# A Fourier transform in front of a mixture of experts: folding the input on VectorE in the first three batches too

## The chip, the cores and the metric

The kernel runs on one core of a Trainium2 chip. The metric is the time of one execution on the device in microseconds (us); lower is better. Three executions of the kernel before took 1033.86, 1037.51 and 1032.04 us, so its median is 1033.86 us.

The core has a TensorE (PE, matrix products, with PEld for its weight loads), a VectorE (DVE), a ScalarE (ACT), a GpSimd (POOL, here only an issuer of indirect transfers) and a SyncE (SP, which issues the other transfers). All transfers run on 16 shared DMA engines.

## The reference

The first half takes the real part of a two-dimensional Fourier transform of `x` (8 batches x 2496 positions x 256 features). The second half sends every one of the 19968 resulting rows to one of 8 experts and applies that expert's two matrices:

```python
X = np.fft.fft(x, axis=1); X = np.fft.fft(X, axis=2); x = X.real
logits = x @ w_gate + modality_bias[modality_id]
e_idx = np.argmax(logits, axis=1)
probs = softmax(logits); gate_w = probs[np.arange(N), e_idx]
for e in range(E):                       # 8 experts, D = 256, F = 1024
    mask = e_idx == e
    h = np.maximum(x[mask] @ w1[e], 0.0)
    out[mask] = gate_w[mask, None] * (h @ w2[e])
```

## The kernel before, in words

**A batch.** Each of the 8 batches `b` passes through four steps. `load_x` brings its input in two halves `c` into the tile `XM`. A half holds, for each of its five positions, the input itself (index 0) and its mirrored part (index 1); the two have to be added, since the real part of the transform needs only their sum. `XM` has two buffers, so the next batch's halves can only be loaded when this batch's first step has read them. `fold` then prepares a half, `stage1` multiplies it with a cosine and sine table (L533 to L541), and `stage23` goes through 11 groups `g`: one product into `T2` (L570), a copy by ACT (L512), a second product with the table `e3` (L585), and an eviction that makes a rounded f16 row on ACT (L516) and its remainder on DVE (L517, with the logits copied by L593). `route` computes expert, gate and destination of every row (L630 to L682; the destinations are the tile `dsti`), and 22 indirect transfers of POOL write the rows to the table `xd`, sorted by expert (`scatter`, L708).

**The mirrored half.** In batches below `UB` = 3 the sum is made by TensorE: `stage1` issues two accumulating products for each position (L538, L539), one on each part, and ACT squares both parts to find a scale (L394). In later batches DVE adds the two parts (L397), ACT squares the sum (L398), and `fold` halves the features again.

**The experts.** A block takes 256 rows of one expert: `xT<-xd` reads them transposed (L1077), L1096 is the first product, L1101 (ACT) and L1102 (DVE) split the result in two f16 tiles, L1116 is the second product, L1124 and L1125 write the rows out. The first three blocks need the rows of batch 0 only, the next 13 those of batches 0 and 1, and so on. Blocks start when the first step of batch 2 is through; from there on TensorE alternates between blocks and the remaining batches.

**The weights.** The 16 weight matrices ("units", two for each expert) are split in two f16 halves by the kernel itself: `wload` brings a unit into a buffer `wa` (four buffers), `wfold` folds it on DVE (L834, L835, even units only), `wnorm` finds its scale (16 small products L848 and DVE steps), `whi` rounds on ACT (L869), `wlo` takes the remainder on DVE (L876), and `wstore` writes the result to memory. Units 0 to 5 are made between the steps of batches 0 and 1.

**What sets the order.** A planner orders every engine's instructions when the program is built. `issue_after(x)` keeps what it encloses behind the instruction `x`; `behind` gives a piece of weight work a low priority and such conditions. Names used in them: `m2t` is the last product of `prep_m2`, which makes the tables `m2u`; `acted` and `mark` are the last eviction on ACT and on DVE; `head` is the end of a step of `route`; `expi` is its exponential; `plused` is the first piece of the rows' tails. An engine runs its list strictly in order: an instruction that waits holds all behind it. SP's list holds the loads, the stores of converted weights and the reads `xT`, in one order.

Of the kernel before, what the change touches and what calls it, by code (L numbers as in the profile page):

```python
# [12 lines left out]
F16 = mybir.dt.float16  # L13
# [60 lines left out]
UB = 3  # L74
RV = 1
# [168 lines left out]
class Kernel:  # L244
# [141 lines left out]

    def fold_add(self, b, c):
        n = 4 if b < UB else 2
        if c == 0:
            self.sq = self.fft.tile([P, n], F32, name=f"nst{n}")  # L390
        if b < UB:
            jk = self.wp.tile([P, NH * D], F16, name="xj", bufs=1)
            for h in range(2):
                self.nc.scalar.activation(jk.rearrange("p (i d) -> p i d", i=NH), self.XM[c][:, h], AF.Square, accum_out=self.sq[:, 2 * c + h:2 * c + h + 1])  # L394
            return
        X = self.XM[c][:, 0]
        self.nc.vector.tensor_tensor(X, X, self.XM[c][:, 1], ALU.add)  # L397
        self.nc.scalar.activation(self.XM[c][:, 1], X, AF.Square, accum_out=self.sq[:, c:c + 1])  # L398
# [56 lines left out]
    def scale(self, b):  # L455


        rt = self.rt
        V = self.nc.vector
        eb = rt.tile([P, 1], F32, name="xeb")  # L460
        s = rt.tile([P, 1], F32, name="xsc")
        inv = rt.tile([P, 1], F32, name="xinv")
        self.pow2(self.total(self.sq, self.psf.tile([P, 512], F32, name="psf")), eb, s, 204 if b >= FB else 188, 2.0 if b < UB else 1.0)
        V.tensor_scalar(inv.bitcast(I32), eb.bitcast(I32), float(66 << 23), None, ALU.add)
        il = None
        if b >= FB:
            il = rt.tile([P, 1], F32, name="xil")
            V.tensor_scalar(eb.bitcast(I32), eb.bitcast(I32), float(56 << 23), None, ALU.add)
            V.tensor_tensor(il, eb, self.ml, ALU.mult)
        self.xs, self.nxt = s, (s, il, inv)  # L470

    def fold(self, b, c):
# [11 lines left out]
        if b < UB:  # L484
            self.PQ = self.XM[c][:, :, :, 0:P], self.XM[c][:, :, :, P:D]
            return
# [32 lines left out]
    def stage1(self, b, c):  # L519
# [3 lines left out]
        for h, src in enumerate(self.PQ):  # L523
# [3 lines left out]
            for i0, n in ((0, 3), (3, 2)):  # L527
# [4 lines left out]
                for i in range(n):  # L532
                    o = v[:, :, 12 * i:12 * i + 12]  # L533
                    if b >= FB:
                        for k, (a, w) in enumerate(HL):
                            nc.tensor.matmul(o, src[:, a, i0 + i, :], self.c1h[:, w, i1 + i, :], start=k == 0, stop=k == 2)  # L536
                    elif b < UB:
                        for k in range(2):  # L538
                            self.staged = nc.tensor.matmul(o, src[:, k, i0 + i, :], self.c1[:, i1 + i, :], start=k == 0, stop=k == 1).ins  # L539
                    else:  # L540
                        nc.tensor.matmul(o, src[:, i0 + i, :], self.c1[:, i1 + i, :], start=True, stop=True)  # L541
# [201 lines left out]
    def stream(self):  # L743
# [13 lines left out]
        for b in range(B):  # L757
# [4 lines left out]
            for g, _ in enumerate(self.stage23(b)):  # L762
# [3 lines left out]
                if g == 0 and b + 1 == FB:  # L766
                    self.m2_split()
# [5 lines left out]
                yield self.at(b)  # L773
            if b + 1 == FB:
# [3 lines left out]
            for step in (ORDER0, ORDER1, ORDER2, ORDER)[min(b, 3)]:  # L778
# [4 lines left out]
                elif step == "s":  # L783
                    next(s, None)
                elif step == "f":
                    with ExitStack() as x:
                        if b == 1:
                            x.enter_context(self.tc.issue_after(self.head))
                        if b == 0:
                            x.enter_context(self.tc.issue_after(self.acted))  # L790
                        self.fold(b + 1, 0)
                elif more:
                    with ExitStack() as x:
# [3 lines left out]
                        if b == 0:  # L797
                            x.enter_context(self.tc.issue_after(self.expi))
                        self.fold(b + 1, 1)
# [357 lines left out]
def fft_moe(ctx, tc, t):  # L1157
# [31 lines left out]
    behind(both(k.whi, 0, 1), k.acted)  # L1189
    behind(both(k.wlo, 0, 1))  # L1190
    both(k.wstore, 0, 1)()
    both(k.wload, 4, 5)()
    steps(12 - WHI)
    steps(7)
    behind(both(k.wnorm, 2, 3))
# [124 lines left out]
```

## Time and profile before

| | |
|---|---|
| three executions | 1033.86, 1037.51, 1032.04 us; median 1033.86 |
| the profiled execution | 1035.88 us, of which the span is 1034.1 us |
| PE busy | 1000.7 us (97%) |
| DVE, ACT, POOL busy | 540.5 us (52%), 443.5 us (43%), 367.6 us (36%) |
| chain that ended last | PE 69%, issue 12%, DMA 10%, POOL 4%, DVE 2%, ACT 2% |

The profile gives the execution in 40 slices, the transfers by queue, the instructions by line, and the chain of work that ended last: followed back from the last instruction, at each step to what released it. A busy share is a mean over the whole span. The change lies in the first 90 us, so the stretches there have to be read by themselves.

### The profile page before, as it was taken

The numbers are of one execution on the slowest core, as the hardware profiler recorded it, in microseconds if no ns is written. First come the engines' busy times: TensorE is split into PE (matmuls) and PEld (weight loads), VectorE is DVE, ScalarE is ACT, GpSimd is POOL, SyncE is SP. The second block draws the span as 40 slices with busy tenths as digits, with TensorE's granted clock in tenths as the row PEclk, the third lists the DMA queues.
The fourth block names the chain that finished last, engine by engine and source line by source line (L and its number), as shares of the span: only waits on it lengthen the run. The fifth ranks groups of instructions, "written<-read, shape, count | busy, mean of one in ns | idle before, by whom it ended". The sixth has DMA issues, their size and how long they took to land.

```text
span 1034.1 us, 25844 instructions
## 1 busy us (share of the span) xinstructions
PE 1000.7 (97%) x9910; PEld 904.4 (87%) x9910; DVE 540.5 (52%) x1577; ACT 443.5 (43%) x870; POOL 367.6 (36%) x351
## 2 busy tenths in 40 slices
PE   6989899999999999999999999999999999999996
PEld 6878788898998889999999998888888888889896
DVE  2859866576857558779754347423232322222221
ACT  4775566555643354455533333333232323233232
POOL 0077822135414441744344334335351212121111
PEclk9999999999999999999999999999999999999999
DMA  9837969278558958989766963897788895594891
GB/s 327 332 137 234 363 167 287 58 236 249 166 139 284 321 157 236 287 250 304 233 182 200 248 184 76 260 262 241 174 235 235 255 257 175 159 294 137 225 207 35
DMA packets 149725, 227.65 MB, mean 220 GB/s; under 512 B 116309, under 2 KB 117375, under 8 KB 132695
## 3 DMA queue, kind: packets, MB, share of 16 engines
q1 hardware_dynamic: 133031, 183.75, 61.1%
q0 software_dynamic: 16560, 42.15, 11.8%
q8 instruction: 80, 1.31, 0.5%
q14 instruction: 54, 0.44, 0.2%
HBM read 191.77 MB, written 62.48 MB: 246 GB/s over the span
## 4 chain that ended last, share of the span: by engine, by line
PE 69%; issue 12%; DMA 10%; POOL 4%; DVE 2%; ACT 2%; SPq 1%; POOLq 0%; ACTq 0%
PE psm L1096 30%; PE pso L1116 30%; DMA wa<-w 5%; DMA XM<-x 3%; POOL out L1125 3%; PE psf L565 2%; PE psf L583 2%; PE psf L570 2%; PE psf L536 1%; POOL xd L708 1%; PE psf L585 1%; DMA pack<-c_pack 1%; PE psf L539 1%; DMA xT<-xd 1%; DVE w L876 1%
## 5 line engine op out<-in xcount | busy, mean ns | idle before, releaser
L1096 PE MATMUL psm<-xT,w 128*128 128x256 f16 (+1 forms) x4368 | 454.4, 261 | 10.2 <-DVE H L1102 5.8
L1116 PE MATMUL pso<-w,H 128*128 128x256 f16 x3864 | 450.5, 273 | 0.9 <-ACT ob L1124 0.9
L1096 PEld LDWEIGHTS <-w 128*128 128x128 f16 x4368 | 384.3, 98 | 49.9 <-issue 8.4
L1116 PEld LDWEIGHTS <-H 128*128 128x128 f16 x3864 | 375.3, 98 | 43.7 <-issue 1.1
L1102 DVE SCALAR_TENSOR_TENSOR H<-psm,H 128x512 f16<-128x512 f32 x322 | 219.8, 687 | 334.6 <-ACT H L1101 334.0
L1125 POOL DMA_INDIRECT out<-ob,ig x161 | 164.7, 1023 | 516.9 <-ACT ob L1124 486.8
L1101 ACT ACTIVATE H<-psm 128x512 f16<-128x512 f32 x322 | 190.5, 596 | 229.9 <-PE psm L1096 227.1
L1124 ACT ACTIVATE ob<-pso,gs 128x256 f32<-128x256 f32 x161 | 68.6, 471 | 247.0 <-PE pso L1116 207.5
L708 POOL DMA_INDIRECT xd<-rp,dsti x88 | 101.4, 1152 | 94.3 <-DVE rm L228 49.9
L708 POOL DMA_INDIRECT xd<-rm,dsti x88 | 92.9, 1055 | 41.9 <-issue 18.5
L517 DVE SCALAR_TENSOR_TENSOR T<-psf,T 120x280 f16<-120x280 f32 (+2 forms) x95 | 43.4, 463 | 42.3 <-ACT T L516 42.2
L876 DVE SCALAR_TENSOR_TENSOR w<-wa,wsc,w 128x1024 f16<-128x1024 f32 x32 | 39.9, 1276 | 9.4 <-ACT w L869 9.3
L516 ACT ACTIVATE T<-psf 120x280 f16<-120x280 f32 (+2 forms) x95 | 38.8, 422 | 10.5 <-PE psf L536 5.7
L570 PE MATMUL psf<-m2u,T 128*120 128x280 f32 x132 | 37.2, 403 | 2.2 <-DVE Lg L593 1.5
L539 PE MATMUL psf<-c,XM 128*128 128x132 f32 x240 | 31.5, 294 | 7.0 <-DMA c<-c_c 6.9
L539 PEld LDWEIGHTS psf<-c,XM 128*128 128x128 f32 x240 | 30.4, 204 | 7.1 <-DMA XM<-x 6.9
L583 PE MATMUL psf<-T,pack 120*128 120x145 f16 x330 | 34.7, 224 | 1.5 <-DVE T L517 1.5
L869 ACT ACTIVATE w<-wa,wsc 128x1024 f16<-128x1024 f32 (+1 forms) x24 | 33.4, 1425 | 4.3 <-DVE wsc L405 3.5
L565 PE MATMUL psf<-pack,T 128*120 128x144 f16 (+1 forms) x330 | 31.5, 229 | 0.0
L512 ACT COPY T<-psf 120x280 f32<-120x280 f32 (+2 forms) x57 | 22.7, 407 | 17.1 <-PE psf L570 8.2
L855 ACT ACTIVATE xj<-wa 128x1024 f16<-128x1024 f32 x20 | 21.1, 1054 | 18.0 <-DVE wa L834 9.1
L516 ACT ACTIVATE rp<-psf 128x256 f16<-128x256 f32 x55 | 21.1, 383 | 15.8 <-PE psf L583 11.8
(186 smaller groups left out, 598.0 us busy)
## 6 DMA issues: line engine op xcount, KB each, us to landing
w<-w SPq DMA_DIRECT2D x80, 1028.0 KB
w<-w SPq DMA_DIRECT2D x80, 1024.0 KB
XM<-x SPq DMA_DIRECT2D x14, 1280.0 KB
wa<-w SPq DMA_DIRECT2D x16, 1024.0 KB
out<-ob,ig POOLq DMA_INDIRECT x161, 7.1
XM<-x SPq DMA_DIRECT2D x2, 768.0 KB
xT<-xd SPq DMA_TRANSPOSE x91
xd<-rp,dsti POOLq DMA_INDIRECT x88, 5.2
```

The lines of the kernel that those rows point to most:

```text
L516: self.acted = self.nc.scalar.activation(dst[:, 0], ps, AF.Identity, scale=scale).ins
L539: self.staged = nc.tensor.matmul(o, src[:, k, i0 + i, :], self.c1[:, i1 + i, :], start=k == 0, stop=k == 1).ins
L565: nc.tensor.matmul(oh, T1[h][:, a, g, :], self.m2h[h][:, w], start=h + k == 0, stop=h * k == 2, skip_group_check=True)
L570: nc.tensor.matmul(ps[0:120, 0:280], T1[h][:, g, :], self.m2u[h], start=h == 0, stop=h == 1)
L583: nc.tensor.matmul(ps3[0:P, cols], self.e3h[:, a, j, :], T2[:, w, cols], start=k == 0, stop=k == 2)
L708: i = self.nc.gpsimd.indirect_dma_start(out=self.t["xd"], out_offset=bass.IndirectOffsetOnAxis(ap=at, axis=0), in_=row, in_offset=None, bo ...
L1096: l1 = nc.tensor.matmul(ps[:, q, :], w1v[:, h, kt, ft], xT[:, xs, :], start=k == 0, stop=k == 5).ins
L1101: nc.scalar.activation(H[:, 0, f0:f0 + NF, :], ps, AF.Relu)
L1102: self.mark = V.scalar_tensor_tensor(H[:, 1, f0:f0 + NF, :], ps, 0.0, H[:, 0, f0:f0 + NF, :], ALU.max, ALU.subtract).ins
L1116: nc.tensor.matmul(po[:, tg, :], H[:, hh, ft, tg * P:(tg + 1) * P], w2v[:, wh, ft, :], start=k == 0, stop=k == 23)
L1124: self.ob = nc.scalar.activation(ob, po[:, tg, :], AF.Identity, scale=gs[:, tg:tg + 1]).ins
L1125: ins = nc.gpsimd.indirect_dma_start(out=t["out"], out_offset=bass.IndirectOffsetOnAxis(ap=ig.bitcast(I32)[:, tg, 0:1], axis=0), in_=ob, i ...
```

## The change

The input is folded by DVE in all batches, and the second product of `stage1` and the second square per half are gone. For batch 0 the four parts are added as they are (`PARTS`); for batches 1 and 2 the additions stand behind groups 7 and 9 of the previous batch's `stage23` (`ADDS`), and the squares in front of the previous batch's `route`. `m2_split`, which makes the f16 tables for batches 3 to 7, stands behind batch 0's `stage23`. Unit 1 (the second matrix of expert 0) is converted behind batch 0's routing; its scale is still found before.

```diff
+    def add(self, c, *parts):
+        for i0, i1 in parts or ((0, NH),):
+            X = self.XM[c][:, 0, i0:i1]
+            self.nc.vector.tensor_tensor(X, X, self.XM[c][:, 1, i0:i1], ALU.add)
...
     def fold_add(self, b, c):
-        n = 4 if b < UB else 2
         if c == 0:
-            self.sq = self.fft.tile([P, n], F32, name=f"nst{n}")
-        if b < UB:
-            jk = self.wp.tile([P, NH * D], F16, name="xj", bufs=1)
-            for h in range(2):
-                self.nc.scalar.activation(jk.rearrange("p (i d) -> p i d", i=NH), self.XM[c][:, h], AF.Square, accum_out=self.sq[:, 2 * c + h:2 * c + h + 1])
-            return
+            self.sq = self.fft.tile([P, 2], F32, name="nst")
         X = self.XM[c][:, 0]
-        self.nc.vector.tensor_tensor(X, X, self.XM[c][:, 1], ALU.add)
+        if b >= UB:
+            self.add(c)
+        elif b == 0:
+            self.add(c, *PARTS)
         self.nc.scalar.activation(self.XM[c][:, 1], X, AF.Square, accum_out=self.sq[:, c:c + 1])
...
-                    elif b < UB:
-                        for k in range(2):
-                            self.staged = nc.tensor.matmul(o, src[:, k, i0 + i, :], self.c1[:, i1 + i, :], start=k == 0, stop=k == 1).ins
                     else:
-                        nc.tensor.matmul(o, src[:, i0 + i, :], self.c1[:, i1 + i, :], start=True, stop=True)
+                        self.staged = nc.tensor.matmul(o, src[:, i0 + i, :], self.c1[:, i1 + i, :], start=True, stop=True).ins
...
-                if g == 0 and b + 1 == FB:
-                    self.m2_split()
+                if b + 1 < UB and g in ADDS:
+                    with self.tc.issue_after(self.mark):
+                        self.add(ADDS.index(g))
...
+            if b == 0:
+                with self.tc.issue_after(self.acted), self.tc.issue_after(self.mark):
+                    self.m2_split()
...
+                elif step == "f" and b + 1 < UB:
+                    with self.tc.issue_after(self.acted if b == 0 else self.head):
+                        self.fold(b + 1, 0)
+                        self.fold(b + 1, 1)
+                    self.parts(0)
...
-    behind(both(k.whi, 0, 1), k.acted)
-    behind(both(k.wlo, 0, 1))
-    both(k.wstore, 0, 1)()
-    both(k.wload, 4, 5)()
+    behind(both(k.whi, 0), k.acted)
+    behind(both(k.wlo, 0))
+    k.wstore(0)
+    k.wload(4)
     steps(12 - WHI)
     steps(7)
+    behind(both(k.whi, 1), k.expi)
+    behind(both(k.wlo, 1), k.plused, k.head)
+    k.wstore(1)
+    k.wload(5)
```

On DVE, in the second half of batch 0's `stage23`, the list before read as follows (`w2_0_107` is the converted unit 1, the `rp` are rows, `wsc` and `web` scales):

```order
L859 TENSOR_SCALAR web_315<-web_315 128x1
L878 TENSOR_TENSOR w2_0_107<-web_287,web_315 128x1
L517 SCALAR_TENSOR_TENSOR rp_405<-psf_402,xsc_167,rp_405 128x256
L593 COPY Lg_245<-psf_402 128x16
L876 SCALAR_TENSOR_TENSOR w2_0_107<-wa_208,wsc_316,w2_0_107 128x1024 x2
L517 SCALAR_TENSOR_TENSOR rp_405<-psf_414,xsc_167,rp_405 128x256
```

The same place now (`XM_312` and `XM_314` are the halves of batch 1):

```order
L596 COPY Lg_223<-psf_373 128x16
L391 TENSOR_TENSOR XM_312<-XM_312 128x1280
L411 TENSOR_SCALAR wsc_294<-web_293 128x1
L523 SCALAR_TENSOR_TENSOR rp_376<-psf_386,xsc_157,rp_376 128x256
L596 COPY Lg_223<-psf_386 128x16
L870 TENSOR_SCALAR web_293<-web_293 128x1
L523 SCALAR_TENSOR_TENSOR rp_376<-psf_397,xsc_157,rp_376 128x256
L596 COPY Lg_223<-psf_397 128x16
L391 TENSOR_TENSOR XM_314<-XM_314 128x1280
```

The two remainders of unit 1 have left this place, and the two additions of batch 1 stand in it.

On DVE, where the `rm` rows (the mirrored outputs) of batch 0 are made behind its routing, the list before ended thus, with the fold of unit 4 (L834) as the last:

```order
L228 TENSOR_SCALAR rm<-rp 128x2x2x127
L614 TENSOR_TENSOR bias<-mf,mb 128x176
L615 TENSOR_TENSOR btmp<-mid,mb 128x176
L917 TENSOR_TENSOR sp_st_3_1155<-sp_st_3_1155,sp_ok_3_1153 1x8
L925 SCALAR_TENSOR_TENSOR sp_nd_3_1161<-sp_ok_3_1153,done_99 1x3
L834 TENSOR_TENSOR wa<-wa 128x1024
```

And now:

```order
L229 TENSOR_SCALAR rm<-rp 128x2x2x127
L928 TENSOR_TENSOR sp_st_3_1105<-sp_st_3_1105,sp_ok_3_1103 1x8
L936 SCALAR_TENSOR_TENSOR sp_nd_3_1111<-sp_ok_3_1103,done_99 1x3
L619 TENSOR_TENSOR bias<-bias,btmp 128x176
L887 SCALAR_TENSOR_TENSOR w_0_107<-wa,wsc,w_0_107 128x1024 x2
L889 TENSOR_TENSOR w_0_107<-web 128x1
L845 TENSOR_TENSOR wa<-wa 128x1024
```

The two remainders of unit 1 now stand directly in front of the fold of unit 4.

On SP, the list before between the converted unit 0 (`w_0_104`) and the first table of blocks (`sp_i`):

```order
L883 DMA w<-w_0_104 128x4096
L826 DMA wa<-w 128x2048
L883 DMA w<-w_0_107 128x4112
L826 DMA wa<-w 128x2048
L385 DMA XM<-x 128x2x1280 x2
L1064 TENSOR_LOAD sp_i_1164
```

And now:

```order
L894 DMA w<-w_0_104 128x4096
L837 DMA wa<-w 128x2048 x2
L894 DMA w<-w_0_107 128x4112
L386 DMA XM<-x 128x2x1280 x2
L1075 TENSOR_LOAD sp_i_1114
```

The loads of units 4 and 5 are now neighbours. Unit 5 goes into the buffer of unit 1, so its load, the store of unit 1 and the loads of batch 2's input behind them all stand behind the conversion of unit 1.

## Rows read from the trace of the kernel before

**Rows 1.** Stretches: us; busy us and count of each engine; granted clock, DMA share, GB/s.

```profile
20.50:42.60 22.10, 20.14 (x136) 16.54 (x136) 16.82 (x45) 14.20 (x28) 0.00 (x0) 1.00 0.90 358
...
51.30:85.40 34.10, 30.62 (x243) 26.09 (x243) 22.86 (x117) 24.73 (x45) 23.71 (x23) 1.00 0.37 124
85.40:140.00 54.60, 49.93 (x399) 42.65 (x398) 44.17 (x116) 31.51 (x63) 43.70 (x28) 0.97 0.89 301
140.00:1034.10 894.10, 877.88 (x8960) 797.11 (x8957) 445.13 (x1229) 355.20 (x696) 299.35 (x295) 1.00 0.73 212
```

**Rows 2.** Chain of waits, 50 to 140 us: start, duration in us, and what.

```profile
51.71 7.32 DMA XM<-x
...
79.75 2.39 DMA xd<-rm,dsti
82.36 1.37 SPq L1077
...
89.14 6.86 DMA XM<-x
96.01 28.02 DMA wa<-w
...
131.79 4.46 DMA xT<-xd
136.30 3.76 PE psm L1096 x33
```

**Rows 3.** Timeline of PE: start, us, engine, line, what; idle time before in brackets.

```profile
6.90 7.25 PE L539 MATMUL psf<-c,XM 128*128 128x132 f32 x40 [6.90 <-DMA c<-c_c]
...
41.27 4.68 PE L539 MATMUL psf<-c,XM 128*128 128x132 f32 x40
...
85.63 1.58 PE L1096 MATMUL psm<-xT,w 128*128 128x256 f16 x13
```

**Rows 4.** Timeline of ACT around the conversion of unit 1 and the squares.

```profile
36.14 1.99 ACT L869 ACTIVATE w<-wa,wsc 128x2048 f16<-128x2048 f32 x1
...
41.85 1.26 ACT L394 ACTIVATE xj<-XM 128x1280 f16<-128x1280 f32 x1
43.01 0.19 ACT L394 ACTIVATION_READ_ACCUMULATOR xj<-XM 128x1 f32 x1
```

**Rows 5.** Timeline of DVE from the first weights to batch 0's destinations.

```profile
20.47 1.23 DVE L834 TENSOR_TENSOR wa<-wa 128x1024 f32<-128x1024 f32 x1 [0.82 <-DMA wa<-w]
...
38.16 2.48 DVE L876 SCALAR_TENSOR_TENSOR w<-wa,wsc,w 128x1024 f16<-128x1024 f32 x2 [1.32 <-ACT w L869]
...
41.98 0.48 DVE L517 SCALAR_TENSOR_TENSOR rp<-psf,xsc,rp 128x256 f16<-128x256 f32 x1
42.38 0.16 DVE L593 COPY Lg<-psf 128x16 f32<-128x16 f32 x1
...
50.20 0.18 DVE L682 CAST dsti<-dst 128x22 int32<-128x22 f32 x1
```

**Rows 6.** Timeline of POOL: batch 0's scatters, then two of batch 1's.

```profile
51.32 1.17 POOL L708 DMA_INDIRECT xd<-rp,dsti  x1 [49.89 <-DVE rm L228]
52.80 0.97 POOL L708 DMA_INDIRECT xd<-rp,dsti  x1 [0.30 <-issue]
54.07 1.70 POOL L708 DMA_INDIRECT xd<-rp,dsti  x1 [0.30 <-ACT T L512]
...
79.75 1.03 POOL L708 DMA_INDIRECT xd<-rm,dsti  x1 [0.30 <-issue]
84.75 10.30 POOL L708 DMA_INDIRECT xd<-rp,dsti  x1 [3.97 <-ACT T L512]
...
100.22 1.78 POOL L708 DMA_INDIRECT xd<-rp,dsti  x1 [0.30 <-issue]
```

**Rows 7.** Timeline of DVE beside those scatters.

```profile
53.70 1.21 DVE L834 TENSOR_TENSOR wa<-wa 128x1024 f32<-128x1024 f32 x1
...
84.50 3.65 DVE L876 SCALAR_TENSOR_TENSOR w<-wa,wsc,w 128x1024 f16<-128x1024 f32 x3
...
99.68 1.47 DVE L397 TENSOR_TENSOR XM<-XM 128x1280 f32<-128x1280 f32 x1
```

More of the change, by code (lines that the diff above doesn't have):

```diff
@@ L74 @@
 UB = 3
+ADDS = 7, 9
 RV = 1
@@ L385, in fetch_x, with parts @@
         self.nc.sync.dma_start(self.XM[c][:, :, i0:i1], self.t["x"][b, :, :, NH * c + i0:NH * c + i1])
+    def add(self, c, *parts):
+        for i0, i1 in parts or ((0, NH),):
+            X = self.XM[c][:, 0, i0:i1]
+            self.nc.vector.tensor_tensor(X, X, self.XM[c][:, 1, i0:i1], ALU.add)
+    def parts(self, c):
+        self.PQ = tuple(self.XM[c][:, 0, :, i:i + P] for i in (0, P))
     def fold_add(self, b, c):
-        n = 4 if b < UB else 2
         if c == 0:
-            self.sq = self.fft.tile([P, n], F32, name=f"nst{n}")
-        if b < UB:
-            jk = self.wp.tile([P, NH * D], F16, name="xj", bufs=1)
-            for h in range(2):
-                self.nc.scalar.activation(jk.rearrange("p (i d) -> p i d", i=NH), self.XM[c][:, h], AF.Square, accum_out=self.sq[:, 2 * c + h:2 * c + h + 1])
-            return
+            self.sq = self.fft.tile([P, 2], F32, name="nst")
         X = self.XM[c][:, 0]
-        self.nc.vector.tensor_tensor(X, X, self.XM[c][:, 1], ALU.add)
+        if b >= UB:
+            self.add(c)
+        elif b == 0:
+            self.add(c, *PARTS)
         self.nc.scalar.activation(self.XM[c][:, 1], X, AF.Square, accum_out=self.sq[:, c:c + 1])
@@ L462, in scale @@
         inv = rt.tile([P, 1], F32, name="xinv")
-        self.pow2(self.total(self.sq, self.psf.tile([P, 512], F32, name="psf")), eb, s, 204 if b >= FB else 188, 2.0 if b < UB else 1.0)
+        self.pow2(self.total(self.sq, self.psf.tile([P, 512], F32, name="psf")), eb, s, 204 if b >= FB else 188)
         V.tensor_scalar(inv.bitcast(I32), eb.bitcast(I32), float(66 << 23), None, ALU.add)
@@ L484, in fold @@
         if b < UB:
-            self.PQ = self.XM[c][:, :, :, 0:P], self.XM[c][:, :, :, P:D]
+            self.parts(c)
             return
@@ L788, in stream @@
                             x.enter_context(self.tc.issue_after(self.head))
-                        if b == 0:
-                            x.enter_context(self.tc.issue_after(self.acted))
                         self.fold(b + 1, 0)
@@ L796, in stream @@
                         self.bias(b + 1)
-                        if b == 0:
-                            x.enter_context(self.tc.issue_after(self.expi))
-                        self.fold(b + 1, 1)
+                        if b + 1 < UB:
+                            self.parts(1)
+                        else:
+                            self.fold(b + 1, 1)
                     for _ in s:
```

## The prediction

> **What bounds the kernel now.** I read the stretches first, then the chain of waits, then the timelines of single engines. In the last 894 us TensorE is busy for 877.88 us [rows 1]: it idles 16 us there, so whatever shifts the start of that stretch shifts the end by as much. What TensorE does before is another matter. Between 51.3 and 85.4 us it idles 3.5 us, and between 85.4 and 140 us another 4.7 us, while the DMA engines are 89% busy [rows 1]. The chain of waits shows who is waited for there, and hardly a link of it is a product of `stage1`: batch 0's last scatter starts at 79.75 us and has landed at 82.14, SP issues the first read `xT` at 82.36, and, because SP's list is in order, the load of batch 3's input only at 89.14; a weight load issued at 96.01 us then lands at 124.03, and the read for the second set of blocks, issued at 131.79, lets TensorE go on at 136.30 [rows 2]. TensorE's first block starts at 85.63 us [rows 3], 3.3 us after the first read was issued. So the first 136 us are set by the moment at which batch 0's 22 scatters are through, and behind that by transfers queued in SP's order. That moment is the sum of three steps: the end of batch 0's `stage23` on VectorE (42.54 us), its routing up to the destinations (50.38 us) [rows 5], and POOL's scatters (51.32 to 80.78 us) [rows 6].
>
> **The change, part by part.** *Products and squares removed.* The 40 records of 20 products take 4.68 us in batch 1 and 7.25 us at the very start [rows 3]; 120 records go, so TensorE loses 3 x 4.68 = 14 us of work or a little more. ACT loses six squares of 1.26 + 0.19 us [rows 4], 8.7 us. Both lie before 85.6 us, where neither engine sets the end. Their gain is worth only what it takes off the three steps; I cost it there and nowhere else.
>
> *Batch 0 up to the end of `stage23`.* VectorE, idle at the start, adds the four parts as they arrive; TensorE has half the products, and may begin `stage23` up to about 3 us earlier. But the first weights still land at 20.47 us [rows 5], and from there on VectorE has the folds, the remainders of unit 0 and 22 evictions in one list. It was busy for 16.82 of the 22.1 us up to 42.6 [rows 1]. From this list the two remainders of unit 1 go (2.48 us, and a wait of 1.32 us ahead of them for ACT's rounding, itself 1.99 us [rows 4, 5]), and two additions of 1.47 us [rows 7] come: 16.82 - 2.48 + 2.94 = 17.3 us of work. With no idle time left it would end at 37.8 us, with all of the 5.3 us kept at 43.1 us. I take 41.3 us, 1.2 us earlier than now, since most of the idle time is waiting for evictions that ACT and TensorE hand over one group at a time, and the additions stand between these.
>
> *Routing of batch 0.* It took 50.38 - 42.54 = 7.84 us. Into its list on VectorE come the eight steps of `m2_split`, the four of batch 1's scale and one of a weight's scale. The trace has such steps at 0.16 us (the small copy) and 0.48 us (the eviction) [rows 5]; eight small and five large ones are 3.7 us at most, and below nothing is excluded, because the routing is a closed row of dependent steps on the same engine. On ACT the two squares of batch 1 (2.9 us) stand ahead of a rounding that `m2_split` needs on VectorE. Overlap lets me take 1.9 us. The destinations then come at 41.3 + 7.84 + 1.9 = 51.0 us, 0.6 us later than now.
>
> *The scatters of batch 0.* A scatter takes 0.97 us and the next follows after 0.30 [rows 6]. The one at 54.07 us took 1.70 us and ended at 55.77, 0.86 us after the fold (53.70 + 1.21 us) in which it began; the one at 100.22 us took 1.78 us and ended 0.85 us after an addition like those that are added here (99.68 + 1.47 us); and the one at 84.75 us, which began in a row of remainders, took 10.30 us [rows 6, 7]. So a scatter that begins while such a step runs waits for its end. Where the fold of unit 4 stood alone, 2.48 us of remainders now stand in front of it: 3.7 us in a row. A scatter begins somewhere in it, on the mean half a spacing (0.64 us) after its start: a wait of 3.1 us instead of 0.73, that is 2.3 us more. The two additions for batch 2, which also fall among these scatters, cost 1.47 - 0.64 = 0.8 us each. Together 4.0 us; the bounds are 0 (each scatter begins just ahead of such a step) and 3.7 - 0.73 + 2.94 = 5.9 us. The first read comes 0.6 + 4.0 = 4.6 us later, at 87.0 us, and TensorE's first block near 90.2 us.
>
> The Trainium skill, "SBUF — State Buffer", section "Who interferes with whom", says that a VectorE step with two inputs in SBUF contends with GpSimd instructions that read SBUF, and infers that writing descriptors needs only the write side, so that additions would leave such transfers alone. By that inference the 4.0 us would be 0; the scatters at 54.07 and 100.22 us say otherwise. It is the second rival below.
>
> *What stands in SP's list.* Unit 5's load, the store of unit 1 and batch 2's input now wait for unit 1's remainders. These end near 51.0 + 6.3 = 57.3 us (the `rm` rows and small steps stand between). 1.05 + 1.05 + 2.62 MB (from the tiles' shapes) at the 358 GB/s of the stretch from 20.5 us [rows 1] are 13.2 us: batch 2's second half lands near 70.5 us, where it landed at 59.03 [rows 2]. Its addition stands behind group 9 of batch 1's `stage23`, which VectorE reaches near 72 us. I cost this at nothing; the slack is 1.5 us.
>
> *What comes through.* Everything behind the first reads in SP's order moves by 4.6 us, up to the read of 131.79 us. The other condition of that read, batch 1's scatters, began at 84.75 us and stood 10.30 us in the remainders; they now begin near 87 us, in the same remainders, so about 2 us later. TensorE's 4.7 idle us in this stretch can take up a little. Between 2 and 4.6 us I take 4.0, near the chain that ended last. Behind 140 us nothing gives it back.
>
> **Sum.** The profiled execution was 1035.88 us, 2.0 us above the median but within the runs. 1035.88 + 4.0 = 1039.9 us for it, and 1033.86 + 4.0 = **1037.9 us** for the median, 0.4% slower: within the 0.5% (5.2 us) that a measurement of this kernel can tell from no change.
>
> **Rivals.** *Batch 2's input comes too late (slower).* The place is SP's list behind unit 1. If the 4.7 MB move at 250 GB/s rather than 358, they need 18.9 us, the second half lands at 76.2 us, and VectorE stands 4 us in the middle of the evictions of batch 1. Its routing, its scatters and the read of 131.79 us follow: 4.6 + 4 = 8.6 us less what TensorE's idle time absorbs, some 1041.5 us. It decides from a landing later than 72 us. For it: the transfers were 90% busy in this part of the kernel before 42.6 us; against it: only 37% from 51.3 to 85.4 us [rows 1].
>
> *Additions and remainders leave the scatters alone.* Then 0.6 us is all: 1034.5 us. Against it are the rows above.
>
> *The early start comes through (faster).* If VectorE works without idle time, batch 0's `stage23` ends at 37.8 us; if `m2_split` hides in the routing, the destinations come at 45.6 us, 4.7 us earlier; if few scatters are held, the reads follow 4 to 6 us earlier, and TensorE has the work taken away to let it. Less the steps of `m2_split` that no longer stand between the first blocks, that is some 6 us: 1028 us. For it: 5.3 us idle on VectorE in that stretch [rows 1], and a wait of 1.32 us that goes with unit 1. Against it: three things have to hold together.
>
> **How the numbers follow.** The forecast has a chance of 0.50, with a range of its own from 1035 to 1041 us; 0.38 of it lies within 0.5% and 0.12 above. The late input has 0.24, the scatters left alone 0.10, the early start 0.16. So faster 0.16, within 0.5% 0.38 + 0.10 = 0.48, slower 0.12 + 0.24 = 0.36. The range that leaves out no more than a tenth at either side reaches from 1030 to 1043 us.
>
> **What would show it.** In the changed kernel's profile: batch 0's last eviction on VectorE near 41 us and its destinations near 51 us; one scatter of about 4 us beside the remainders of unit 1 and two of 1.5 to 2.4 us beside the additions; the first `xT` issued near 87 us and TensorE idle for some us ahead of its first block; the second set of blocks near 140 us; no wait of the additions for batch 2's input. Destinations before 47 us, or scatters of 0.97 us throughout, would make it wrong on the fast side; an addition that waits over 2 us for its input on the slow side.

## The result and the profile after

Over 20 executions each the changed kernel takes 1040.66 us (1037.59 to 1045.36) and the kernel before 1034.86 us (1032.04 to 1037.75): a ratio of 1.0056, 95% interval 1.0044 to 1.0067. The forecast was +4.0 us, the result is +5.8 us. Medians and ratios, here and in the table of the experiments, leave out three executions that took far longer than the others of their kernel (1212.63 us of e2_u1only, 2674.98 us of e5_u1back_rp6, 4106.49 us of the kernel before). The profiled execution of the changed kernel took 1038.10 us, the third fastest of its 20 and only 2.2 us above the profiled one of before; the rows below can account for those 2.2 us, and not for the other 3.6.

The stretches of the changed kernel, with the columns of [rows 1]: length, busy us (and count) of PE, PEld, DVE, ACT and POOL, granted clock, DMA share, GB/s.

```profile
20.50:42.60 22.10, 19.57 (x131) 16.24 (x130) 20.02 (x59) 15.32 (x38) 0.00 (x0) 0.96 0.84 333
42.60:51.30 8.70, 8.69 (x80) 7.73 (x78) 7.71 (x45) 5.14 (x11) 2.09 (x3) 0.90 0.05 16
51.30:85.40 34.10, 24.28 (x151) 20.07 (x152) 20.92 (x79) 20.36 (x36) 24.41 (x20) 0.90 0.63 217
85.40:140.00 54.60, 49.32 (x386) 42.66 (x385) 44.16 (x130) 30.36 (x59) 42.67 (x28) 0.94 0.88 297
140.00:1036.20 896.20, 881.21 (x8984) 799.40 (x8981) 447.98 (x1235) 357.23 (x702) 300.12 (x295) 1.00 0.73 212
```

Against [rows 1], VectorE idles 2.1 us up to 42.6 us instead of 5.3, the DMA engines all but stand still from 42.6 to 51.3 us (16 GB/s) and carry 217 instead of 124 GB/s in the stretch behind, and TensorE idles 9.8 us there instead of 3.5. Its granted clock, a mean over the two levels 1.2 and 2.4 GHz, is below full (1.00) in all four stretches up to 140 us; before, it was so only in the fourth, at 0.97. Behind 140 us it is 1.00 in both, but TensorE has 8984 records of products left there instead of 8960.

VectorE of the changed kernel (start, us, engine, line, what; idle time before in brackets), against [rows 5, 7]:

```profile
38.53 0.47 DVE L523 SCALAR_TENSOR_TENSOR rp<-psf,xsc,rp 128x256 f16<-128x256 f32 x1
38.92 0.16 DVE L596 COPY Lg<-psf 128x16 f32<-128x16 f32 x1
...
47.51 0.16 DVE L685 CAST dsti<-dst 128x22 int32<-128x22 f32 x1
...
51.43 2.46 DVE L887 SCALAR_TENSOR_TENSOR w<-wa,wsc,w 128x1024 f16<-128x1024 f32 x2
...
53.89 1.20 DVE L845 TENSOR_TENSOR wa<-wa 128x1024 f32<-128x1024 f32 x1
...
65.01 0.48 DVE L523 SCALAR_TENSOR_TENSOR rp<-psf,xsc,rp 128x256 f16<-128x256 f32 x1 [6.37 <-ACT rp L522]
...
72.14 1.48 DVE L391 TENSOR_TENSOR XM<-XM 128x1280 f32<-128x1280 f32 x1
...
75.31 1.49 DVE L391 TENSOR_TENSOR XM<-XM 128x1280 f32<-128x1280 f32 x1 [0.24 <-DMA XM<-x]
```

Batch 0's `stage23` ends at 39.08 us and its destinations stand at 47.67, 3.5 and 2.7 us earlier than before. The row at 65.01 is new: 6.37 us in which VectorE waits for ACT's half of the same row (`rp`).

POOL of the changed kernel, against [rows 6]:

```profile
48.60 1.12 POOL L711 DMA_INDIRECT xd<-rp,dsti  x1 [47.17 <-DVE btmp L618]
50.02 0.97 POOL L711 DMA_INDIRECT xd<-rp,dsti  x1 [0.30 <-issue]
51.30 4.68 POOL L711 DMA_INDIRECT xd<-rp,dsti  x1 [0.30 <-ACT T L518]
...
72.97 1.50 POOL L711 DMA_INDIRECT xd<-rm,dsti  x1 [0.30 <-issue]
...
76.05 1.60 POOL L711 DMA_INDIRECT xd<-rm,dsti  x1 [0.31 <-issue]
...
80.53 0.97 POOL L711 DMA_INDIRECT xd<-rm,dsti  x1 [0.30 <-issue]
88.21 9.23 POOL L711 DMA_INDIRECT xd<-rp,dsti  x1 [6.71 <-ACT T L518]
```

The scatter of 51.30 takes 4.68 us and ends 0.89 us after the fold (53.89 + 1.20), the last of a row of remainders and fold; those of 72.97 and 76.05 lie across the two additions. Batch 0's train takes 32.9 us (48.60 to 81.50) instead of 29.5.

The chain of waits of the changed kernel (start, us, what), against [rows 2]:

```profile
50.80 0.40 ACT T L518
...
51.30 13.11 DMA xd<-rp,dsti
...
65.31 1.30 PE psf L588 x4
...
78.61 3.97 ACT w L880 x3
82.58 1.25 ACT XM L404 x2
...
84.64 3.84 PE psf L544 x20
88.48 2.82 PE psm L1107 x24
...
93.90 16.07 DMA wa<-w
...
133.22 3.84 DMA xT<-xd
...
137.11 2.93 PE psm L1107 x13
```

The held scatter needs 13.11 us to land. Of these, 4.68 are the hold on POOL. The other 8.4 fall together with the load of unit 5, the store of unit 1 and batch 2's input, which waited for unit 1's remainders and go out together from 54 us on. The trace has the landing of every scatter: the one of 56.28 us, held by nothing (0.97 us on POOL), lands 8.80 us after its start, while the two of 48.60 and 50.02 us, ahead of those loads, landed after 2.59 and 2.45. So the landing is stretched without a hold too. Batch 1's second buffer `rp` is the one from which the held scatter reads (five buffers, four used by batch 0). So ACT and VectorE stand until 64.4 us, batch 1's `stage23` ends at 78.9 us instead of 76.5, and three roundings and a square on ACT hold the last products ahead of the first block. The first read `xT` is no longer what the first block waits for.

TensorE ahead of the first block, in the changed kernel:

```profile
84.50 3.98 PE L544 MATMUL psf<-c,XM 128*128 128x132 f32 x20
88.27 4.00 PE L1107 MATMUL psm<-xT,w 128*128 128x256 f16 x33
```

and at the same place before:

```profile
80.91 4.77 PE L539 MATMUL psf<-c,XM 128*128 128x132 f32 x40
```

Half of the products now take 3.98 instead of 4.77 us, and no wait stands ahead of the block, which starts at 88.27 us (before: 85.63 [rows 3]). The granted clock was 0.61 from 84.5 to 88.3 us, and 1.00 from 80.9 to 85.6 us before.

A second profiled execution of the same kernel, taken beside the experiments (1037.83 us), has the steps later: last eviction ending at 41.00, destinations at 49.59, the scatter 4.67 us long, the idle row 5.80 us. SP and PE in it:

```profile
86.19 1.37 SPq L1088 DMA_TRANSPOSE xT<-xd  x1
```

```profile
85.96 3.86 PE L544 MATMUL psf<-c,XM 128*128 128x132 f32 x20
89.61 3.56 PE L1107 MATMUL psm<-xT,w 128*128 128x256 f16 x28
```

VectorE takes up the first half `H` of the second set of blocks at 138.43 us in the kernel before, at 141.97 and 142.85 in the two profiles of the changed one. The ways there differ. TensorE's first product of that set starts at 136.30 us before, at 137.11 in the first profile and at 139.97 in the second. In the first profile TensorE had idled 3.93 us for the read, and the clock stood at the lower level behind it:

```profile
137.10:139.10 2.00, 1.99 (x10) 1.44 (x10) 1.79 (x8) 2.00 (x4) 1.70 (x2) 0.50 1.15 194
```

Its first 36 products took 5.45 us there, against 4.09 before and in the second profile.

### The profile page after: what moved, and what is told of

It reads as the page before. It is cut to its first block, busy times and chain, and to the rows that moved or that the text cites. A ratio compares the mean times of both kernels' runs of the same rounds, so it can differ in the third digit from the quotient of the medians.

```text
span 1036.2 us, 25588 instructions
## 1 busy us (share of the span) xinstructions
PE 994.1 (96%) x9784; PEld 895.4 (86%) x9784; DVE 548.1 (53%) x1585; ACT 436.2 (42%) x858; POOL 370.1 (36%) x351
## 4 chain that ended last, share of the span: by engine, by line
PE 68%; issue 12%; DMA 11%; POOL 3%; ACT 2%; DVE 2%; SPq 1%; POOLq 0%; ACTq 0%; DVEq 0%
PE psm L1107 30%; PE pso L1127 29%; DMA XM<-x 3%; DMA wa<-w 3%; POOL out L1136 2%; PE psf L573 2%; DMA xd<-rp,dsti 2%; PE psf L568 2%; PE psf L586 2%; DMA xd<-rm,dsti 1%; PE psf L542 1%; PE psf L588 1%; PE psf L544 1%; ACT w L880 1%; POOL xd L711 1%
## 5 line engine op out<-in xcount | busy, mean ns | idle before, releaser
L711 POOL DMA_INDIRECT xd<-rp,dsti x88 | 105.0, 1194 | 93.0 <-DVE btmp L618 47.2
L391 DVE TENSOR_TENSOR XM<-XM 128x1280 f32<-128x1280 f32 (+2 forms) x18 | 24.1, 1337 | 24.4 <-DMA XM<-x 24.4
L544 PE MATMUL psf<-c,XM 128*128 128x132 f32 x120 | 22.4, 355 | 9.6 <-DVE XM L391 7.7
L544 PEld LDWEIGHTS psf<-c,XM 128*128 128x128 f32 x120 | 20.3, 256 | 12.5 <-DVE XM L391 7.2
L588 PE MATMUL psf<-T,pack 120*128 120x145 f32 (+1 forms) x132 | 23.3, 296 | 5.8 <-ACT T L518 5.7
```

The costliest lines, as they stand in the source:

```text
L544: self.staged = nc.tensor.matmul(o, src[:, i0 + i, :], self.c1[:, i1 + i, :], start=True, stop=True).ins
L711: i = self.nc.gpsimd.indirect_dma_start(out=self.t["xd"], out_offset=bass.IndirectOffsetOnAxis(ap=at, axis=0), in_=row, in_offset=None, bo ...
```

## The experiments

Theory P (pile-up): unit 1 behind the routing holds a scatter and bunches the transfers, and the wait for `rp` carries that to the end. Theory A: only the hold of the scatters counts. Theory C: the lost products let TensorE idle and its clock fall. Three chips (I, II, III) took the twelve runs. Ratios are to the kernel before on the same chip; the clock is the mean over the executions.

| run | chip | this, us | before, us | ratio, 95% interval | clock, this / before |
|---|---|---|---|---|---|
| c_after | I | 1043.09 | 1036.1 | 1.0066, 1.0045 to 1.0087 | 0.986 / 0.996 |
| e1r_u1back | I | 1043.34 | 1036.1 | 1.0072, 1.005 to 1.0094 | 0.987 / 0.996 |
| e3r_rp6 | I | 1042.33 | 1036.1 | 1.0066, 1.0044 to 1.0089 | 0.986 / 0.996 |
| e5_u1back_rp6 | I | 1044.48 | 1036.1 | 1.0082, 1.0055 to 1.0108 | 0.986 / 0.996 |
| e1_u1back | II | 1084.67 | 1086.9 | 0.9984, 0.997 to 0.9998 | 0.972 / 0.978 |
| e2_u1only | II | 1098.80 | 1086.9 | 1.0117, 1.0097 to 1.0137 | 0.973 / 0.978 |
| e3_rp6 | II | 1083.46 | 1086.9 | 0.9978, 0.9953 to 1.0003 | 0.973 / 0.978 |
| e4_xm2first | II | 1090.63 | 1086.9 | 1.0047, 1.0027 to 1.0068 | 0.971 / 0.978 |
| e6_u1back_710 | III | 1088.37 | 1085.9 | 1.0023, 1.0002 to 1.0044 | 0.970 / 0.977 |
| e7_rp6_68 | III | 1086.37 | 1085.9 | 1.0002, 0.9985 to 1.002 | 0.971 / 0.977 |
| e8_twice_610 | III | 1095.58 | 1085.9 | 1.008, 1.0054 to 1.0106 | 0.974 / 0.977 |
| e9_adds_710 | III | 1095.57 | 1085.9 | 1.0088, 1.0065 to 1.0111 | 0.967 / 0.977 |

On chips II and III the kernel before itself takes 4.8 to 4.9% longer than on chip I. The profiles taken there, all of changed versions, have stretches in which ScalarE starts nothing and for whose end the profile names no cause. The chain of waits of e8_twice_610 has the longest:

```profile
68.22 0.39 ACT T L518
68.62 18.72 another core or an unknown queue
```

Its engines in that stretch, in the columns of [rows 1]:

```profile
68.60:87.30 18.70, 1.71 (x8) 1.13 (x8) 0.84 (x6) 0.02 (x1) 12.11 (x13) 0.66 0.56 215
```

Only POOL's scatters and the transfers go on. The chain of e1_u1back has three in a row:

```profile
67.55 6.20 another core or an unknown queue
...
74.24 3.06 another core or an unknown queue
...
77.77 5.34 another core or an unknown queue
```

They lie just where the disputed waits of 3 to 6 us lie, and differ from kernel to kernel. Of these three chips, the changed kernel unedited ran on chip I alone. So the times of chips II and III are told, but no theory is decided by them; what they are used for is the clock ahead of 50 us, where no such stretch has yet come (the earliest begins at 59.88 us).

**Unit 1 back (e1_u1back, e1r_u1back).**

```diff
-    behind(both(k.whi, 0), k.acted)
-    behind(both(k.wlo, 0))
-    k.wstore(0)
-    k.wload(4)
+    behind(both(k.whi, 0, 1), k.acted)
+    behind(both(k.wlo, 0, 1))
+    both(k.wstore, 0, 1)()
+    both(k.wload, 4, 5)()
...
-    behind(both(k.whi, 1), k.expi)
-    behind(both(k.wlo, 1), k.plused, k.head)
-    k.wstore(1)
-    k.wload(5)
```

> The changed kernel with one part undone: unit 1's conversion, store and the next load stand again beside unit 0's; the additions on VectorE and the early M2 split stay. Theory P (pile-up): what the change loses comes from unit 1 behind the routing. It holds the scatter of 51.30 for 4.68 us and sends the store, the load and batch 2's input into the DMA engines just while that scatter lands (13.1 us), so batch 1's fourth rp buffer comes 6.4 us late. P expects no wait of 6 us before batch 1's fourth group of evictions, its second stage's end back at 77 us or earlier, first block products at 85.6 or earlier, and 1031 to 1035.5 us, no slower than the kernel before. Theory C (clock): the loss comes from the half of the stage-1 products that is gone, because TensorE idles more ahead of the blocks and is granted a lower clock. C expects the granted clock of 42.6 to 85.4 us still near 0.9 and 1038 to 1041 us.

> The changed kernel with unit 1 converted beside unit 0 again, on the same chip as the changed kernel itself. On the chip of the first four runs ScalarE stood still several times for 3 to 6 us between two instructions with nothing outstanding that the profile shows, so its profile told nothing of waits of that size. Theory P (pile-up behind unit 1) expects 0.4 to 0.8% less than the changed kernel and at most 1.0 of the kernel before, no wait above 2 us for an rp buffer, and the second stage of batch 1 over by 77 us. Theory C (clock, from the products that are gone) expects a time within 0.2% of the changed kernel.

On chip I the waits that theory P names are gone. POOL of e1r_u1back:

```profile
54.58 2.23 POOL L711 DMA_INDIRECT xd<-rp,dsti  x1 [0.30 <-ACT rp L522]
...
82.10 0.97 POOL L711 DMA_INDIRECT xd<-rm,dsti  x1 [0.31 <-issue]
...
114.69 0.97 POOL L711 DMA_INDIRECT xd<-rm,dsti  x1 [0.30 <-issue]
```

None of batch 0's scatters takes over 2.3 us, VectorE idles at most 1.2 us ahead of an `rp` eviction, batch 1's `stage23` ends at 74.7 us, and its scatters are through at 115.7 us (before: 129.1). But TensorE gains nothing by it. Its first block, which P expected at 85.6 us or earlier, starts later than in the changed kernel, and waits for the first read `xT` (issued at 84.64 us; 82.36 before):

```profile
89.47 6.33 PE L1107 MATMUL psm<-xT,w 128*128 128x256 f16 x36 [4.78 <-DMA xT<-xd]
```

The granted clock was 0.62 from 89.47 to 95.6 us; the same 36 products took 4.09 us in the kernel before. The read for the second set goes out no earlier than before either (131.79 us), though the scatters are through 13 us sooner; here the chain of waits leads to it through a weight load:

```profile
100.56 25.51 DMA wa<-w
```

```profile
132.04 1.29 SPq L1088 DMA_TRANSPOSE xT<-xd  x1
```

VectorE takes up the first `H` of that set at 138.69 us, 0.3 us from the kernel before, but TensorE has 8990 records of products left behind 140 us, as in the changed kernel (8984 and 8996) and not as before (8960). More is lost behind 140 us:

```profile
85.40:140.00 54.60, 46.30 (x364) 39.33 (x364) 43.79 (x107) 29.11 (x55) 29.36 (x25) 0.94 0.89 299
140.00:1047.80 907.80, 886.55 (x8990) 802.61 (x8988) 444.95 (x1235) 355.99 (x701) 304.71 (x297) 0.99 0.72 210
```

The last stretch is 13.7 us longer than in [rows 1]: 8.7 us more busy time of TensorE, 5.0 us more idle (this execution, 1049.6 us, was the slowest of its ten; if the difference to the median 1043.34 lies in this stretch, some 7 us are an estimate for the median). One cause in sight is the planner: with unit 1 back it writes another order for the batches behind. I compared TensorE's products from the first block on, some 9350, row by row as the traces show them (operation, names, shapes): 821 rows differ from the changed kernel's, where only 89 of the changed kernel's differ from those of before. Between the 37th and the 38th `H` of ACT it runs 47 products where there were 12, and batch 2's destinations come at 237.8 us instead of 226.3 (changed kernel: 229.5). How much of the loss is the order's is not shown. So P holds for the waits and falls for the first block and for the time: it expected 0.4 to 0.8% less than the changed kernel, and C's expectation, a time within 0.2% of it, is what came (1043.34 and 1043.09 us). An edit of one part is not an edit of one part when a planner orders the rest.

**Six `rp` buffers (e3_rp6, e3r_rp6).**

```diff
-RPB = 5
+RPB = 6
```

> The changed kernel with six rp buffers instead of five, so that batch 1's fourth group of rows asks for no buffer whose scatters of batch 0 still have to land before; nothing else is edited. Theory P (pile-up, through the rp buffer) expects the wait of 6.37 us at 65.01 gone or under 2 us, batch 1's second stage to end 3 to 6 us earlier than 78.9, the first block then held by the scatters alone (first xT near 82), and 1034 to 1037.5 us. Theory A (only the hold of the scatters counts) expects no change against the changed kernel: 1039.5 to 1041.5 us, since the held scatter of 4.68 us is still there.

> The changed kernel with six rp buffers, on the same chip as the changed kernel itself. Theory P through the rp buffer: the wait of 6.37 us goes, 0.3 to 0.6% less than the changed kernel, about 1.0 of the kernel before. Theory A (only the hold of the scatters counts): within 0.2% of the changed kernel. If the wait goes and the time stays, batch 1's routing was not what set the end, and the hold of the scatters was.

The 6.37 us row is gone, as P says. VectorE of e3r_rp6 then waits for what stood next, batch 2's input:

```profile
71.02 1.49 DVE L391 TENSOR_TENSOR XM<-XM 128x1280 f32<-128x1280 f32 x1 [4.32 <-DMA XM<-x]
...
75.23 1.49 DVE L391 TENSOR_TENSOR XM<-XM 128x1280 f32<-128x1280 f32 x1 [1.27 <-DMA XM<-x]
```

This is the first rival of the prediction at its own place, and it had been hidden only by the longer wait. The second set's first `H` comes at 141.29, 1.6 us earlier than in c_after; the time is the same (1.0066), under another order again (745 rows differ from the changed kernel's). By the words set down for it, a wait that goes and a time that stays speak for theory A; with the order changed as well, that is not shown either.

**Both (e5_u1back_rp6).** The two edits together.

> The changed kernel with both: unit 1 converted beside unit 0 again and six rp buffers. Theory P expects no rp wait even with unit 1 back, so no gain of the sixth buffer over unit 1 back alone: within 0.2% of that kernel, and 0.997 to 1.0 of the kernel before. If the buffer is a wait of its own that the pile-up only made longer, this kernel is 0.2 to 0.4% faster than with unit 1 back alone.

1.0082 beside 1.0072: the sixth buffer gains nothing where unit 1 does not pile up; the order of TensorE's products is the same in both. That half of P's expectation held, the 0.997 to 1.0 did not.

**The changed kernel again (c_after).** No edit.

> The changed kernel itself, unedited, as the yardstick beside the three that follow. All theories expect 1.004 to 1.007 of the kernel before, with the 4.7 us scatter, the rp wait of 6 us and the lower granted clock between 42.6 and 85.4 us again. A time within 0.2% of the kernel before would say that the loss hangs on the chip it runs on.

1.0066, with the 4.67 us scatter, the idle row of 5.80 us and a granted clock of 0.81 and 0.90 in the two stretches from 42.6 to 85.4 us: the loss stays on a chip on which the kernel before takes 1036.1 us.

**Unit 1 alone (e2_u1only).** The kernel before with unit 1's lines (the diff of e1_u1back backwards).

> The kernel before with one part of the change alone: unit 1 converted, stored and its buffer reloaded behind batch 0's routing; the mirrored half still added by matmuls and the M2 split at its old place. Theory P (pile-up) expects a scatter of batch 0 held for 4 us or more beside unit 1's remainders, one that lands in 10 us or more, and a wait of several us for an rp buffer in batch 1's second stage: 1038 to 1043 us. Theory C (clock, from the missing products) expects TensorE as busy as before in 20 to 51 us, a clock of 0.98 or more there, and 1034 to 1036 us.

1.0117 on chip II is above what P expected (1038 to 1043 us are 1.003 to 1.008 of the kernel before) and above C's. The held scatter beside unit 1's remainders took 2.94 us, not 4; the first scatter of batch 1 took 12.68. The clock is 1.00 from 20 to 51.3 us, where every kernel with half the products is below that, so this run loses without C's cause. Its order is not that of before, though (901 rows differ), and its stretches without work (up to 5.90 us) lie where the waits would.

**Batch 2's input first (e4_xm2first).**

```diff
-    k.wstore(1)
-    k.wload(5)
     behind(both(k.wnorm, 2, 3))
     steps(10)
-    behind(both(k.wfold, 4, 5), k.rowed)
+    behind(both(k.wfold, 4), k.rowed)
     steps(12)
+    k.wstore(1)
+    k.wload(5)
+    k.wfold(5)
```

> The changed kernel with unit 1's store and unit 5's load behind batch 2's input in SyncE's list instead of ahead of it; conversion of unit 1 stays behind the routing. Theory P expects the transfers of 51 to 70 us to be spread differently but to be as many: the scatter issued near 51.3 lands in 6 to 10 us instead of 13.1, the rp wait shrinks to 1 to 4 us, 1036 to 1039.5 us. Theory A (only the hold of the scatters counts) expects 1039.5 to 1041.5 us. A third reading, that batch 2's input is what comes late, expects the additions of batch 2 several us earlier and a first block 1 to 2 us earlier.

1.0047 on chip II; its stretches without work (up to 7.29 us) cover the waits in question, and 735 rows of the order differ from the changed kernel's. Inconclusive.

**Four runs with the later order kept.** The places of batch 1's additions (`ADDS`) were chosen so that TensorE's order behind the first blocks stays near that of the changed kernel (27 to 131 rows differ in the traces) or, for the last, of the kernel before (113). e6_u1back_710 is unit 1 back with `ADDS = 7, 10`, e7_rp6_68 six buffers with `ADDS = 6, 8`. The other two:

```diff
 e8_twice_610
-ADDS = 7, 9
+ADDS = 6, 10
...
-                        self.staged = nc.tensor.matmul(o, src[:, i0 + i, :], self.c1[:, i1 + i, :], start=True, stop=True).ins
+                        for k in range(2 if b < UB else 1):
+                            self.staged = nc.tensor.matmul(o, src[:, i0 + i, :], self.c1[:, i1 + i, :], start=True, stop=True).ins
 e9_adds_710 (unit 1's lines as in e1_u1back, and)
-ADDS = 7, 9
+ADDS = 7, 10
...
+                if g == 0 and b + 1 == FB:
+                    self.m2_split()
...
-            if b == 0:
-                with self.tc.issue_after(self.acted), self.tc.issue_after(self.mark):
-                    self.m2_split()
```

> Unit 1 converted beside unit 0 again, as in the second run of that kind, but with batch 1's additions behind the eighth and eleventh group of the second stage (places 7 and 10), because the planner then leaves the order of TensorE's work behind the first blocks as it is in the changed kernel; with 7 and 9 it also rewrote the order of batches 2 and 3, so those runs compared two things at once. Theory P (pile-up behind unit 1) expects the second set of blocks 3 to 5 us earlier than in the changed kernel, and 0.998 to 1.002 of the kernel before. Theory C (the granted clock, lower because TensorE lost half of its stage-1 products) expects the mean clock still near 0.987 and 1.004 to 1.007.

> Six rp buffers again, with the additions at places 6 and 8, which keeps the later order of the changed kernel. Theory P through the rp buffer expects the wait of 6.4 us gone, the second set 1 to 3 us earlier than in the changed kernel, and 1.001 to 1.004 of the kernel before. Theory A (the hold of the scatters alone) and theory C (clock) expect 1.005 to 1.007.

> The changed kernel, unit 1 behind the routing, with each stage-1 product of the first three batches issued twice into the same place, the second overwriting the first, so that TensorE has as many products there as in the kernel before; additions at places 6 and 10, which keeps the later order of the changed kernel. Theory C (clock) expects the granted clock back at 0.99 or more in 20 to 51 us, a mean of 0.993 or more, and 0.999 to 1.002 of the kernel before. Theory P (pile-up) expects the rp wait of some 6 us still there, the second set 2.5 to 5 us late, and 1.004 to 1.008.

> The kernel before with the additions on VectorE alone (half the stage-1 products gone): unit 1 beside unit 0 and the M2 split at its old place; places 7 and 10 keep the later order of the kernel before. Theory P expects no loss, since nothing stands behind the routing: 0.996 to 1.001 of the kernel before. Theory C expects most of the loss to be here: mean clock 0.99 or less, and 1.003 to 1.006.

They came to chip III, so their totals decide little. Taken by their numbers, 1.0002 for six buffers is below P's range (1.001 to 1.004; the interval reaches into it) and below that of A and C; 1.0023 for unit 1 back is just above P's; 1.008 with the products doubled is against C and at the upper end of P's; 1.0088 for the additions alone is against P and above C's. One thing can be read: the clock. A stretch of e8_twice_610, with the products doubled, and then of e9_adds_710, with half of them:

```profile
20.00:42.60 22.60, 18.77 (x124) 15.45 (x125) 16.68 (x41) 13.18 (x32) 0.00 (x0) 1.00 0.84 336
```

```profile
20.00:42.60 22.60, 19.09 (x126) 15.66 (x125) 18.77 (x44) 14.22 (x27) 0.00 (x0) 0.96 0.91 361
```

In 20 to 42.6 us the clock is 0.93 to 0.97 in all eleven profiles with half the products, on all three chips, and 1.00 in the three with all of them (before, e2_u1only, e8_twice_610). So it is the missing products that lower it there. That this makes the time is not shown: from 42.6 to 51.3 us e8_twice_610 falls to 0.80 all the same, its mean (0.974) rises only halfway to that of before, and it is no faster.

No version beats the kernel before on chip I. The held scatter, the stretched landing and the wait for `rp` are shown as waits; that they make the time is not shown, since the two edits that take them away on chip I leave the time where it was and change the order as well.

## Why the prediction was right, step by step

*Products and squares removed.* 14 us of TensorE's work was to go, worked out as 40 records in 4.68 us. The page has TensorE busy 994.1 us instead of 1000.7, 6.6 us less: the 20 records of the row at 84.50 took 3.98 us, under a clock of 0.61. The forecast had costed this gain at nothing outside the three steps, so its sum does not change; that the removed work takes clock with it was in no term.

*The end of `stage23`.* 41.3 us was forecast, 39.08 and 41.00 were measured, inside the bounds of 37.8 and 43.1. VectorE's idle time up to 42.6 us fell from 5.3 to 2.1 us in the first profile and 3.8 in the second.

*The routing.* 9.74 us were forecast (7.84 + 1.9), 8.59 measured in both executions (39.08 to 47.67, 41.00 to 49.59). The steps of `m2_split` cost 0.75 us more than before, not 1.9. The destinations came at 47.67 and 49.59, not 51.0.

*The scatters.* +4.0 us was forecast for the train, +3.4 and +4.6 measured (32.9 and 34.1 us against 29.5). This is the term on which the forecast rested, and its mechanism stands: one scatter of 4.68 us across unit 1's row, and two across the additions (1.50 and 1.60 in one execution, 2.26 and 1.96 in the other). The forecast counted one held scatter in the kernel before, that of 54.07 us; the one of 56.07 took 1.65 us as well, a small error in the sum. The rows also answer the rival from the Trainium skill, "SBUF — State Buffer", section "Who interferes with whom", by whose inference additions would leave these transfers alone: here they do not. The same section has a step with two inputs in SBUF contend with GpSimd instructions that read SBUF; if writing an indirect transfer reads its destinations `dsti` there, that rule covers these rows, but no run here tells whether it does. One-input steps in f16 (the `rm` rows, 49.87 to 51.1 us) left the scatter of 50.02 at 0.97 us.

*The first read and the first block.* 87.0 and 90.2 us were forecast; 83.08 and 88.27 came in one execution, 86.19 and 89.61 in the other. So the path of the forecast, destinations plus scatters, delayed the first read by 0.7 and 3.8 us and not by 4.6. That the first block is near the forecast is luck, for it is late for another reason than the one given: batch 1's `stage23`, late by the `rp` wait, and ACT's list behind it hold TensorE, not the scatters.

*SP's list.* Costed at nothing; this step failed. Batch 2's second half was to land near 70.5 us, and landed at 75.3, beyond the 72 us from which the first rival was to decide. That the additions hardly waited for it (0.24 and 0.60 us) is luck: VectorE came late itself, by the `rp` wait, and with six buffers the wait appears (4.32 and 1.27 us). It was also wrong that the bunched transfers cost nothing else: they stretch the landing of the held scatter to 13.1 us, and with it the turn of the buffer `rp`. I had asked who waits for each transfer of the list and not who waits for the scatters beside it. The rival's rate of 250 GB/s was nearer than 358: the 4.7 MB took 21.2 us, from 54.05 to 75.3, which are 222 GB/s.

*What comes through.* 4.0 us at the second set was forecast, 3.5 and 4.4 measured at its first `H`. In the first profile this is luck in part: the read of that set is 1.4 us late and its first product 0.8, and the rest is the lower clock and VectorE's other work ahead of that `H`; in the second the read is 4.6 us late and the first product 3.7. Counted in work, TensorE has 24 and 36 more records of products left behind 140 us; at 877.88 us for 8960 records [rows 1] these are an estimated 2.4 and 3.5 us. "Nothing gives it back" failed in the profiles: their ends are 2.1 and 1.9 us late, with TensorE idle for 15.0 and 13.3 us behind 140 us instead of 16.2.

*The sum.* 4.0 us against 5.8 (20 executions) and 7.0 (chip I). At 0.56% it is just outside the 0.5% that had the most chance, with an interval (0.44 to 0.67%) that covers both sides. The two profiles lie at the fast end of this kernel's executions, so the rest shows in no trace. What separates the kernels in every execution is the mean granted clock: 0.982 to 0.989 in 30 of the changed kernel, 0.992 to 0.999 in 27 of before. Within each kernel a clock lower by 0.001 goes with 0.5 to 0.7 us more (correlation -0.43 and -0.45), so the gap of 0.010 would go with 5 to 7 us. That fits, but idle time and a lower clock come together in these traces, so neither is shown to be the cause, and the run that gave the products back did not give the time back. In the profiles the lower clock lies ahead of 140 us, where its price is already in the late starts above. So the time was forecast within its range by a path of which only the holds of the scatters came as described; the `rp` wait, the late input and the clock, which were in no term of the sum, made up for destinations that came 1.4 to 3.3 us earlier than forecast. What makes the last 2 to 3 us stays open, and so does how the total divides between the held scatter, the stretched landings and the clock.

## What to carry to other kernels

When transfers are moved behind a step, price not only their own landing but that of everything that lands beside them, and find the buffer whose next user waits for it. Work taken from an engine that is off the critical path is not a gain for certain: TensorE's clock from 20 to 42.6 us fell in every run that took products away, and 20 products then took 3.98 us where 40 had taken 4.77. And where a planner orders the instructions, compare the orders before comparing times, since three edits near the start changed 735 to 821 rows of the order behind, in kernels whose effect under test was 0.5%.

## What was not expected of the hardware

An indirect scatter took 13.1 and 12.5 us from issue to landing in a stretch in which all queues together moved 217 and 215 GB/s; 4.7 us of that were the hold by VectorE. The next scatter, without a hold, took 8.8 and 8.9 us. The last one before the first read of the kernel before, in a stretch of 124 GB/s, took 2.39 us [rows 1, 2].

On two of three chips the kernel before took 1086 to 1087 instead of 1036 us. The profiles of the other versions there have stretches of 2 to 19 us between 60 and 90 us in which ScalarE starts nothing; the longest sum in one kernel is some 22 us, so they are not the whole difference. Their cause stays open.
